# GpSimd in program order in attention, the fifth tile's branch inside w2's first tile, and the maxima's steps listed anew

## The chip, the cores and the metric

The kernel runs on one core of one Trainium2 chip. The time is the device time of one execution in microseconds (us), and the time before is the median of three runs, 1415.97 us (1415.85 to 1416.66).

The core's engines have queues of their own and run side by side: TensorE (PE; its weight loads are PEld), VectorE (DVE), ScalarE (ACT), GpSimd (POOL) and SyncE (SP), which issues most DMAs. A wait between engines is a semaphore.

## What is computed

```python
x = A_x                                     # [1, 2048, 448]
g = sigmoid((x * gate_w).sum(-1, keepdims=True))
# a: attention, 16 heads of 28
q, k, v = (x @ wqkv) split into heads
a = softmax(q @ k.T * 28**-0.5) @ v @ wo
# b: two of eight experts a token, w1[e]: 448 x 1792, w2[e]: 1792 x 448
topk_idx = argsort(-(x @ w_gate))[:, :2]
gates = softmax(topk_val)
for e in range(8):
    b += (gates * (topk_idx == e)).sum(-1) * (silu(x @ w1[e]) @ w2[e])
out = g * a + (1 - g) * b
```

## The kernel before

**Precision.** A product of fp32 numbers is made of three fast matmuls: each operand is split into a high part (a rounded copy, by ScalarE) and a low part (the rest, by GpSimd or VectorE), and high x high, high x low and low x high are added up. So w1, w2, the tokens and the hidden values all have a copy and a subtraction of their own: `w1h`, `w1l`, `w2h`, `w2l`, `xeh`, `xel`, `hh`, `hl`.

**Stages.** First q, k, v and the router are computed and written to DRAM (to about 119 us). Then come the eight experts, in falling order of their token counts (loop at L859). Then attention over 256 units of 4 heads x 512 queries x 128 keys (L1160 on), and the projection by `wo`.

**One expert.** Its tokens are gathered into four tiles of 128 slots, and for experts 0 to 5 a fifth, smaller one (64 slots or fewer, `CTS[e][4]`), which holds tokens only if the count is over 512. The 1792 hidden rows are done in two halves (`hf`) of seven row tiles each. In a half, w1 comes first: 7 row tiles x 2 halves of the slots x 11 matmuls, 154 in all (L898). Then w2: one output tile for each of the four token tiles, 21 matmuls each, 84 in all (L948). In half 1 the tokens of the next expert are transposed in groups of four matmuls (`turn_x`, L749) between w2's matmuls, two groups in the first tile (behind its 6th and 15th) and one in each later one.

**Accumulators.** Two PSUM banks, `acc0` and `acc1`, are used in turn: `accumulator()` switches to the other one and returns it, `other_accumulator()` returns the one that isn't in use and switches nothing. The transpositions of `turn_x` also go to the other one.

**The fifth tile.** Its w1 part is the end of the second slot half. Its w2 part, `last_slots` (L819), stands in a branch `tc.If(cnt > 512)` (L935): 14 matmuls (28 passes, L825) into one bank, two copies of it by ScalarE (L831), and in half 1 two additions by GpSimd (L833) and two DMAs (L834). Before, the branch stands ahead of w2's first tile.

**The maxima.** Attention needs the largest score of each query first. This work is put into the experts' stage, between TensorE's other matmuls: 1024 blocks of 128 queries x 512 keys (L112). A generator hands them out in steps. A step writes six blocks to the PSUM tile `pm` (six banks, one buffer), and a seventh to the accumulator that is not in use, if it got it as a spare bank; VectorE takes the maximum of each (L126 for the seventh, L132 for the others in two instructions). When 16 query columns of a head group are ready, the maxima are gathered (`mg`, L141), and the next step that gets a bank uses it to transpose and store them (`store_max`, L148) and has six blocks.

**Where the steps stand.** The table `STEPS` gives, for each expert and half, the numbers of the matmuls in w1 (1 to 154) and in w2 (1 to 84) behind which a step comes (`behind`, L853). A negative number is a step without a spare bank.

**Who sets the order.** In the experts' stage PE, DVE, ACT and POOL run in program order (`MANUAL_E`), and SP's order is set by the scheduler. In attention only PE and DVE are in program order (L1074); the scheduler orders ACT, POOL and SP.

**Attention.** `scores` computes a unit's scores (L695) into a bank `ps1` and three banks `ps3`, and ScalarE takes the exponentials (L1091, L1092), three units ahead of `values` (L1101), which adds up P x V. Sixteen units of 128 keys make a pass of four heads over 512 queries; `kt` counts the 16. At the end of a pass the result is copied (`osb`, L1105) and `spread_sums` sends the sums through DRAM by eight GpSimd DMAs (L1048, L1051). In the next pass `divide` uses them at kt 6 to 9. `fetch_routed` (L1005) gathers the two expert results of 128 tokens by two GpSimd DMAs (L1009), `routed` adds them up by VectorE at kt 12, and `split_wo` loads and splits a quarter of `wo` (L1001 to L1003).

Of the kernel before, what the change touches and what calls it, by code (L numbers as in the profile page):

```python
# [20 lines left out]
BUSY = 20  # L21


A, B, C = (17, 50, 83, 116, 149), (17, 50, 83, 116, -154), (-4, 28, 61, 94, -124, 148)
F, G, T = (18, 38, 57, 76), (13, 32, 50, 68), (-11, -25, 39, 59, 76)
STEPS = [((C, F), (A, T)), ((A, G), (C, T)), ((A, G), (C, T)), ((B, F), (B, T)), ((B, F), (B, T)), ((B, F), (B, T)),
         ((A, F), (A, T)), ((A, F), ((-13, 39, 72, 105, 138), (9, 28, 47, 67)))]

S, D, H, DH, E, FF = 2048, 448, 16, 28, 8, 1792
NT = S // 128  # L30
# [24 lines left out]
def tile_gated_mha_moe(ctx: ExitStack, tc: tile.TileContext, x, xT, wv, wqk, wo, w1, w2, out):  # L55
# [106 lines left out]
    def tail_twice(xt):  # L162
        nc.scalar.activation(xt[:, D:512], xt[:, 384:D], AF.Copy)
# [24 lines left out]
    def step(bank):  # L188
        if bank and flush:
            store_max(*flush.pop(0), bank)  # L190
        elif bank:
            spare.append(bank)
        next(ms, None)
        spare.clear()
# [505 lines left out]
    with ExitStack() as pb:  # L700
# [36 lines left out]
        def accumulator():  # L737
            turn[0] ^= 1
            return ps.tile([128, 512], F32, name=f"acc{turn[0]}")

        def other_accumulator():
            return ps.tile([128, 512], F32, name=f"acc{turn[0] ^ 1}")
# [75 lines left out]

        def last_slots(e, hf, hs, y):  # L819
            n, w = CTS[e][4], D // 2  # L820
            py = accumulator()
            for f in range(NH):
                w2r = w2t[e * NF + hf * NH + f][2]
                for c in range(2):
                    nc.tensor.matmul(py[64 * c:64 * c + n, 0:w], hs[f][2][:, 0:n], w2r[:, c * w:(c + 1) * w],  # L825
                                     start=f == 0, stop=f == NH - 1)
            r0 = e * CPAD + 512
            yo = sb.tile([128, D], F32, name="yo") if hf else y
            for c in range(2):
                rw = slice(64 * c, 64 * c + n)  # L830
                nc.scalar.activation(yo[rw, 0:w], py[rw, 0:w], AF.Copy)  # L831
                if hf:
                    nc.gpsimd.tensor_tensor(yo[rw, 0:w], yo[rw, 0:w], y[rw, 0:w], op=ALU.add)  # L833
                    nc.gpsimd.dma_start(ys_d[r0:r0 + n, c * w:(c + 1) * w], yo[rw, 0:w])  # L834
# [18 lines left out]
        def behind(places, i):  # L853
            if i in places:
                step(other_accumulator())
            elif -i in places:
                step(None)

        for e in range(E):  # L859
            CT, HC = CTS[e], CAPS[e] // 2  # L860
            later = CTS[e + 1] if e + 1 < E else []
            if len(CT) == 5:
                cnt = nc.values_load(cnt_i[0:1, 0, e:e + 1], min_val=0, max_val=S)
# [5 lines left out]
            ysb = [None] * 5  # L869
            for hf in range(2):  # L870
                hs = []
                lag = None
                w1_steps, w2_steps = STEPS[e][hf]
                for f in range(NH):
# [48 lines left out]
                    xeh, xel = x_tiles()  # L923

                base = e * NF + hf * NH
                for n_k, k in enumerate((4, 0, 1, 2, 3)):
                    if k == 4:
                        if hf == 0 and len(CT) == 5:
                            ysb[4] = sb.tile([128, D], F32, name="ysb", bufs=5)
                        if (e, hf) == (E - 1, 1):  # L930
                            spilled()

                            nc.scalar.activation(sb.tile([128, 1], F32, name="warm", bufs=1), ident[:, 0:1], AF.Exp)
                        if len(CT) == 5:
                            with tc.If(cnt > 512):  # L935
                                last_slots(e, hf, hs, ysb[4])
                        for f in range(NH):
                            fetch_w2(base + f + 9)
                    n = 128
                    cs = slice(k * 128, k * 128 + n)  # L940
                    if k < 4:
                        py = accumulator()
                    i = 0
                    for f in range(NH if k < 4 else 0):
                        hh, hl, ht = hs[f]
                        w2h, w2l, w2r = w2t[base + f]
                        for a, b in ((hh, w2h), (hh, w2l), (hl, w2h)):
                            nc.tensor.matmul(py[:n, 0:D], a[:, cs], b, start=i == 0, stop=i == 3 * NH - 1)  # L948
                            i += 1
                            behind(w2_steps, 3 * NH * (n_k - 1) + i)  # L950
                            if (e, hf, n_k) == (E - 1, 1, 4) and i in (1, 10):
                                first_scores(i == 10)
                        if hf == 1 and e + 1 < E and (f == 1 or f == 4 and n_k == 1):
                            j = n_k if f == 1 and n_k > 1 else f // 4
                            if j < len(later):
                                turn_x(xgs[j], j, later[j], xeh, xel)
                    if hf == 0 and n_k:

                        r0 = e * CPAD + 512 if n_k == 1 else NMAIN + (3 * e + n_k - 2) * 128
                        nc.sync.dma_start(ys_d[r0:r0 + 128], zero_d)  # L960
                    if hf == 0:
                        if k < 4:
                            ysb[k] = sb.tile([128, D], F32, name="ysb", bufs=5)
                            nc.scalar.activation(ysb[k], py[:, 0:D], AF.Copy)
                        if e + 1 < E:
                            for j in {0: (0, 1), 4: ()}.get(n_k, (n_k + 1,)):
                                if j < len(later):
                                    xgs.append(gather(e + 1, j))
                            for j in {0: (), 1: (0, 1)}.get(n_k, (n_k,)):
                                if j < len(later):  # L970
                                    tail_twice(xgs[j][:later[j]])
                    elif k < 4:
                        r0 = e * CPAD + k * 128
                        yo = sb.tile([128, D], F32, name="yo")
                        nc.scalar.activation(yo, py[:, 0:D], AF.Copy)
                        nc.gpsimd.tensor_tensor(yo, yo, ysb[k], op=ALU.add)
                        nc.sync.dma_start(ys_d[r0:r0 + n], yo)

                    free = {0: ((e * NP + 4, 0),), 1: ((e * NP + NP, 0), (e * NP + NP + 1, 2))}[hf]
                    for p, at in free:  # L980
                        if n_k == at:
                            split_w1_high(p, WHOLE)
                            split_w1_low(p, WHOLE)
# [87 lines left out]
                r += n  # L1071
                p += n

    ctx.enter_context(tc.manual_schedule(engines={mybir.EngineType.PE, mybir.EngineType.DVE}))  # L1074
    todo = []
    b1s, halves, ygs = {}, {}, {}
    units = [(g, qc, kt) for g in range(NG) for qc in range(4) for kt in range(NT)]
# [124 lines left out]
```

## Time and profile before

| what | us |
|---|---|
| median of 3 runs | 1415.97 |
| profiled execution | 1420.36 |
| its span | 1418.6 |
| PE busy | 1402.2 |
| ACT busy | 913.5 |
| DVE busy | 799.6 |
| POOL busy | 645.3 |

The span is the stretch from the first to the last instruction of the program; the rest of an execution lies around it. PE counts as busy for 99% of it, but the ends of matmuls are modelled in the profile, and a matmul begins before the one ahead of it has ended. So small losses are to be read from the distance between the starts of two matmuls, and the rows of time (start in us, duration in us, engine, line, operation, output<-input, partitions x elements, and in brackets the idle time before it and who ended it) serve for that.

### The profile page before, as it was taken

How to read it: one execution, taken by the hardware profiler on the slowest of the kernel's cores; microseconds unless marked ns; L12 is line 12 of the kernel's file. 1: busy time of each engine (PE TensorE's matmuls, PEld its weight loads, DVE VectorE, ACT ScalarE, POOL GpSimd, SP SyncE). 2: the span in 40 equal slices, each digit the busy share in tenths (PEclk: the TensorE clock that was granted, in tenths of full speed). 3: DMA queues.
4: the chain of work that ended last, by engine and by line, in shares of the span. 5: the costliest groups of instructions: out<-in, count | busy, mean ns of one | idle time of the engine just before them, and what ended most of it. 6: DMA issues, size and time to landing. Idle time of an engine off the chain costs nothing. (4 is left out here: it accounts for less than half of the span.)

```text
span 1418.6 us, 28718 instructions
## 1 busy us (share of the span) xinstructions
PE 1402.2 (99%) x11028; PEld 935.7 (66%) x11028; DVE 799.6 (56%) x911; ACT 913.5 (64%) x1531; POOL 645.3 (45%) x682
## 2 busy tenths in 40 slices
PE   9999999999999999999999999999999999999999
PEld 8888888878878888888888887333333333333348
DVE  5736777777877787778888886022231122311136
ACT  5335355355445543654445434899999999999981
POOL 2224587487478666875777636221121122121120
PEclk9999999999999999999999999999999999999999
DMA  9886552343233234323442211311421331142103
GB/s 340 285 282 229 154 164 61 107 138 92 77 119 119 64 113 124 110 64 105 136 124 83 70 59 38 87 44 47 124 75 42 95 84 49 42 126 63 33 22 120
DMA packets 106685, 152.81 MB, mean 108 GB/s; under 512 B 17926, under 2 KB 77523, under 8 KB 106032
## 3 DMA queue, kind: packets, MB, share of 16 engines
q1 hardware_dynamic: 97392, 129.86, 29.7%
q0 software_dynamic: 9008, 20.83, 5.1%
q8 instruction: 89, 1.46, 0.4%
q14 instruction: 52, 0.43, 0.1%
q10 hardware_dynamic: 144, 0.23, 0.1%
HBM read 115.99 MB, written 38.02 MB: 109 GB/s over the span
## 5 line engine op out<-in xcount | busy, mean ns | idle before, releaser
L132 DVE TENSOR_REDUCE mp<-pm 128x3 f32<-128x1536 f32 (+3 forms) x307 | 520.0, 1736 | 43.7 <-PE pm L112 43.7
L1092 ACT ACTIVATE P<-ps 128x1536 f32<-128x1536 f32 x254 | 367.9, 1448 | 0.1
L1101 PE MATMUL po<-P,V 128*32 128x512 f32 x2032 | 270.6, 604 | 0.0
L898 PE MATMUL acc<-xeh,w1h 128*128 128x256 f32 (+6 forms) x880 | 252.5, 296 | 0.0
L898 PE MATMUL acc<-xeh,w1l 128*128 128x256 f32 (+6 forms) x880 | 246.4, 289 | 1.1 <-POOL w1l L730 0.9
L695 PEld LDWEIGHTS ps<-Q,Kh 29*128 29x128 f32 x2032 | 78.1, 183 | 216.2 <-ACT P L1091 213.3
L767 POOL TENSOR_TENSOR w2l<-w2r,w2h 128x448 fp32r<-128x448 f32 x112 | 129.2, 1154 | 161.2 <-ACT w2h L761 122.3
L695 PE MATMUL ps<-Q,Kh 29*128 29x512 f32 x2032 | 189.6, 443 | 3.2 <-ACT P L1091 3.0
L898 PE MATMUL acc<-xel,w1h 128*128 128x256 f32 (+6 forms) x660 | 189.6, 287 | 0.0
L898 PEld LDWEIGHTS acc<-xeh,w1h 128*128 128x128 f32 x880 | 165.7, 188 | 25.4 <-issue 25.2
L948 PE MATMUL acc<-w2h,hh 128*128 128x448 f32 x448 | 170.8, 381 | 2.1 <-ACTq L935 1.8
L898 PEld LDWEIGHTS acc<-xeh,w1l 128*128 128x128 f32 x880 | 165.9, 189 | 4.7 <-POOL w1l L730 2.8
L948 PE MATMUL acc<-w2h,hl 128*128 128x448 f32 x448 | 166.8, 372 | 0.5 <-POOL hl L776 0.5
L948 PE MATMUL acc<-w2l,hh 128*128 128x448 f32 x448 | 166.4, 372 | 0.0
L1105 DVE COPY osb<-po 128x512 f32<-128x512 f32 x16 | 11.1, 692 | 264.3 <-PE po L1101 195.7
L902 ACT ACTIVATE hf<-acc 128x256 f32<-128x256 f32 (+6 forms) x224 | 86.3, 385 | 113.9 <-PE acc L898 98.4
L1048 POOL DMA_DIRECT2D sum_d<-osb x64 | 32.3, 522 | 270.5 <-DVE osb L1105 254.5
L1091 ACT ACTIVATE P<-ps 128x512 f32<-128x512 f32 x254 | 151.8, 598 | 5.3 <-PE ps L695 2.3
L730 POOL TENSOR_TENSOR w1l<-w1r,w1h 128x512 fp32r<-128x512 f32 (+1 forms) x88 | 138.1, 1569 | 29.5 <-ACT w1h L724 22.4
L776 POOL TENSOR_TENSOR hl<-hf,hh 128x512 fp32r<-128x512 f32 x112 | 143.9, 1291 | 0.0
L126 DVE TENSOR_REDUCE mp<-acc 128x1 f32<-128x512 f32 x111 | 76.8, 692 | 105.5 <-PE acc L112 98.0
L898 PEld LDWEIGHTS acc<-xel,w1h 128*128 128x128 f32 x660 | 124.5, 189 | 0.9 <-issue 0.7
(214 smaller groups left out, 1989.6 us busy)
## 6 DMA issues: line engine op xcount, KB each, us to landing
w2r<-in_w_dram SPq DMA_DIRECT2D x112, 224.0 KB
w1r<-in_w_dram SPq DMA_DIRECT2D x56, 384.0 KB
ys_d<-zero_d SPq DMA_DIRECT2D x32, 224.0 KB
qkh_d<-hi SPq DMA_DIRECT2D x28, 256.0 KB
qkl_d<-lo SPq DMA_DIRECT2D x28, 256.0 KB
w1r<-in_w_dram SPq DMA_DIRECT2D x112, 64.0 KB
ys_d<-yo SPq DMA_DIRECT2D x32, 224.0 KB
v_d<-v_s SPq DMA_DIRECT2D x16, 256.0 KB
```

The lines of the kernel that those rows point to most:

```text
L126: nc.vector.tensor_reduce(mp[:, o:o + 1], banks[0], axis=AX.X, op=ALU.max)
L132: nc.vector.tensor_reduce(mp[:, (o + lo) % 256:(o + lo) % 256 + hi - lo], pm[:, lo:hi], axis=AX.X, op=ALU.max)
L695: nc.tensor.matmul(banks[j], k[rw, ks], q[rw, c], start=i == 0, stop=i == 2)
L730: nc.gpsimd.tensor_tensor(l[:, :, half], r[:, :, half], h[:, :, half].bitcast(F32), op=ALU.subtract)
L767: nc.gpsimd.tensor_tensor(w2l, w2r, w2h.bitcast(F32), op=ALU.subtract)
L776: nc.gpsimd.tensor_tensor(hl, hf32, hh[:, 0:512].bitcast(F32), op=ALU.subtract)
L898: nc.tensor.matmul(pu[:, 0:HC], a, b[:, cs], start=i == 0, stop=i == len(mms) - 1)
L902: nc.scalar.activation(hf32[:, hs_], pu[:, 0:nh], AF.Silu)
L948: nc.tensor.matmul(py[:n, 0:D], a[:, cs], b, start=i == 0, stop=i == 3 * NH - 1)
L1091: nc.scalar.activation(P[:, 0], p1, AF.Exp, scale=SCALE)
L1092: nc.scalar.activation(P[:, 1:4], p3, AF.Exp, scale=SCALE)
L1101: nc.tensor.matmul(po[32 * j:32 * j + 32], v[:, kt % 8, 32 * j:32 * j + 32], P[:, j] if n > 1 else P[j], start=kt == 0, stop=kt == NT - 1)
```

## The change

Three edits. `STEPS` is listed anew, 152 places instead of 154. The fifth tile's branch moves from ahead of w2's first tile to behind its third matmul, and its product goes to the accumulator that is not in use instead of the next one in turn; so w2's first tile takes the accumulator that the fifth tile had, and every later tile the other one of the two. The whole split of a pair of w1 (`split_w1_high` and `split_w1_low` with WHOLE) and the loads of w2 stand ahead of the branch in the program. And in attention GpSimd keeps the program's order.

```diff
-A, B, C = (17, 50, 83, 116, 149), (17, 50, 83, 116, -154), (-4, 28, 61, 94, -124, 148)
-F, G, T = (18, 38, 57, 76), (13, 32, 50, 68), (-11, -25, 39, 59, 76)
-STEPS = [((C, F), (A, T)), ((A, G), (C, T)), ((A, G), (C, T)), ((B, F), (B, T)), ((B, F), (B, T)), ((B, F), (B, T)),
-         ((A, F), (A, T)), ((A, F), ((-13, 39, 72, 105, 138), (9, 28, 47, 67)))]
+STEPS = [
+    (([17, 50, 83, 116, 148], [13, 32, 51, 70]), ([7, 39, 72, -100, -124, 148], [-11, -25, 39, 59, 76])),
+    (([17, 50, 83, 116, 149], [18, 38, 57, 76]), ([17, 50, 83, 116, 148], [-11, -25, 39, 59, 76])),
+    (([17, 50, 83, 116, 149], [18, 38, 57, 76]), ([17, 50, 83, 116, 148], [-11, -25, 39, 59, 76])),
+    (([17, 50, 83, 116, 149], [18, 38, 57, 76]), ([17, 50, 83, 116, 148], [-11, -25, 39, 59, 76])),
+    (([17, 50, 83, 116, 149], [18, 37, 56, 75]), ([17, 50, 83, 116, 148], [-11, -25, 39, 59, 76])),
+    (([17, 50, 83, 116, 149], [18, 37, 56, 75]), ([17, 50, 83, 116, 148], [-11, -25, 39, 56, 75])),
+    (([17, 50, 83, 116, 149], [18, 37, 56, 75]), ([17, 50, 83, 116, -149], [-11, -25, 39, 56, 75])),
+    (([17, 50, 83, 116, 148], [15, 34, 53, 72]), ([-12, 39, 72, 105, 138], [9, 28, 47, 67])),
+]
...
         def last_slots(e, hf, hs, y):
             n, w = CTS[e][4], D // 2
-            py = accumulator()
+            py = other_accumulator()
...
+                def fifth():
+                    if len(CT) == 5:
+                        with tc.If(cnt > 512):
+                            last_slots(e, hf, hs, ysb[4])
+
                 for n_k, k in enumerate((4, 0, 1, 2, 3)):
...
-                        if len(CT) == 5:
-                            with tc.If(cnt > 512):
-                                last_slots(e, hf, hs, ysb[4])
                         for f in range(NH):
                             fetch_w2(base + f + 9)
...
                             i += 1
+                            if n_k == 1 and i == 3:
+                                fifth()
                             behind(w2_steps, 3 * NH * (n_k - 1) + i)
...
-    ctx.enter_context(tc.manual_schedule(engines={mybir.EngineType.PE, mybir.EngineType.DVE}))
+    ctx.enter_context(tc.manual_schedule(
+        engines={mybir.EngineType.PE, mybir.EngineType.DVE, mybir.EngineType.Pool}))
```

## The prediction

> **What bounds the kernel now.** I read the busy time by stage first, then who makes TensorE wait, then the order of time around each place that the change touches.
>
> ```profile
> core 0: us, PE busy (x) PEld busy (x) DVE busy (x) ACT busy (x) POOL busy (x), PEclk, DMA share, GB/s
> 119.00:883.00 764.00, 756.28 (x5142) 629.64 (x5140) 600.62 (x498) 370.37 (x909) 518.22 (x454) 1.00 0.35 104
> 903.00:1377.00 474.00, 473.35 (x4968) 164.60 (x4967) 105.39 (x185) 471.58 (x497) 91.38 (x148) 1.00 0.24 64
> ```
>
> From 119 to 883 us (experts) TensorE is busy 756 of 764 us; from 903 to 1377 (attention) ScalarE is busy 471.6 of 474. The first stage follows TensorE's stream and what holds it up, the second follows the exponentials. All three edits work on small holes in these two streams.
>
> ```profile
> PE pm L112 <- DVE mp L132: 2.3, 5, 0.6
> PE pm L112 <- DVE lo L609: 0.9, 1, 0.9
> PE acc L898 <- POOL w1l L730: 0.9, 2, 0.7
>   PEld pm L112: 2.6, 9
> ```
>
> The last row, from the list of who waited on tile mp, adds nine weight loads of the maxima that also waited for VectorE. Matmul ends are modelled, so I measure a wait as the distance between starts, against an undisturbed place. Undisturbed, with a spare bank (seven score blocks, TensorE then VectorE):
>
> ```profile
> 177.28 0.29 PE L898 MATMUL acc<-xel,w1h 128*128 128x288 f32 x1
> 177.41 0.29 PE L898 MATMUL acc<-xeh,w1l 128*128 128x288 f32 x1
> 177.64 0.49 PE L112 MATMUL acc<-khg,qg 28*128 28x512 f32 x1
> 178.30 0.40 PE L898 MATMUL acc<-xeh,w1h 128*128 128x288 f32 x1
> 178.54 0.29 PE L898 MATMUL acc<-xel,w1h 128*128 128x288 f32 x1
> 178.17 0.69 DVE L126 TENSOR_REDUCE mp<-acc 128x1 f32<-128x512 f32 x1 [1.56 <-PE acc L112]
> 178.77 3.42 DVE L132 TENSOR_REDUCE mp<-pm 128x3 f32<-128x1536 f32 x2
> ```
>
> From 177.41 to 178.54 are 1.13 us where two pitches of 0.13 would be 0.26: a step costs TensorE 0.87 us. VectorE has read all of its banks at 178.77 + 3.42 = 182.19, 4.55 us after the step began. The tile pm has one buffer, so the next step must lie some 4.7 us behind. Two blocked places, each behind a step without a spare bank (six blocks):
>
> ```profile
> 394.09 0.29 PE L898 MATMUL acc<-xel,w1h 128*128 128x276 f32 x1
> 394.31 0.49 PE L112 MATMUL acc<-khg,qg 28*128 28x512 f32 x1
> 394.65 0.73 PE L112 MATMUL pm<-khg,qg 28*128 28x512 f32 x6
> 395.54 0.29 PE L898 MATMUL acc<-xeh,w1h 128*128 128x276 f32 x1
> 585.06 0.73 PE L112 MATMUL pm<-khg,qg 28*128 28x512 f32 x6
> 586.10 0.44 PE L948 MATMUL acc<-w2h,hh 128*128 128x448 f32 x1 [0.31 <-ACTq L935]
> 586.58 0.37 PE L948 MATMUL acc<-w2h,hl 128*128 128x448 f32 x1
> 586.79 0.37 PE L948 MATMUL acc<-w2h,hh 128*128 128x448 f32 x1
> 587.40 0.60 PE L749 MATMUL acc<-ident,xg 128*128 128x128 f32 x4
> 587.76 0.45 PE L948 MATMUL acc<-w2h,hh 128*128 128x448 f32 x1
> 589.40 0.73 PE L112 MATMUL pm<-khg,qg 28*128 28x512 f32 x6 [0.39 <-DVE mp L132]
> ```
>
> The first takes 395.54 - 394.09 = 1.45 us, 0.32 more than undisturbed. The second shows the rule for six blocks: 589.40 - 585.06 = 4.34 us. So after a seven-block step TensorE needs 4.7 us of other work, after a six-block step 4.35, or it waits.
>
> **The maxima's steps.** With 0.13 us a w1 matmul (about 0.12 in the last experts, whose tiles have 256 columns instead of 288: an estimate by columns), 0.207 a w2 matmul (586.58 to 586.79), 0.87 for the step itself and 0.4 for a group of four transpositions (587.40 to 587.76), the old lists miss these distances at five kinds of places. (a) 24 matmuls behind a six-block step (-4 to 28, -124 to 148; three halves): 24 x 0.13 + 0.87 = 3.99 against 4.35; six places, 0.32 in the row above and less where w1 is wider, 1.5 in sum. (b) 32 to 50: 18 x 0.207 + 0.87 = 4.60 against 4.7, two places, 0.2. (c) The last w1 step to -11 in w2: 0.39 by the row for each of experts 3 to 5; for expert 6, 5 x 0.12 + 11 x 0.207 + 0.4 + 0.87 = 4.15 against 4.7; 1.7 in sum. (d) 76 to 17 of the next half: 8 x 0.207 + 17 x 0.12 + 0.87 = 4.57 against 4.7; nine places, 1.2. (e) Last expert, 76 to -13 and -13 to 39: 4.09 against 4.7 and 3.99 against 4.35, 1.0. Sum 5.6 us.
>
> In the new lists most of these are gone: 75 to 17 has 9 x 0.207 + 17 x 0.12 + 0.87 = 4.77; 148 to -11 has 6 x 0.125 + 11 x 0.207 + 0.4 + 0.87 and the branch, some 4.6 against 4.7; 72 to -12 has 12 x 0.207 + 12 x 0.12 + 0.87 = 4.79. Left are -100, -124 and 148 in expert 0 (24 to 28 matmuls apart, 0.7 in sum), some 0.2 at -11 in experts 3 to 5, 0.2 in expert 6, 0.24 at -12 to 39, and I add 0.3 for the transpositions of maxima (L148), which now come 16 to 19 matmuls behind a step and need its VectorE work too: 1.6. The pair -25 to 39 is the same in both lists and left out. Saved 4.0.
>
> Counted out over the 1024 blocks, the old lists hold 154 steps, the new 152, since 118 instead of 110 have a spare bank: 2 x 0.87 = 1.7 saved. The first step moves from place 4 to 17, past the one wait for `low`:
>
> ```profile
> 120.87 0.80 PE L112 MATMUL pm<-khg,qg 28*128 28x512 f32 x6 [0.94 <-DVE lo L609]
> ```
>
> Thirteen matmuls later it has nothing to wait for: 0.9 saved. Together 6.6 us.
>
> What is late next is GpSimd.
>
> ```profile
> L776 POOL TENSOR_TENSOR hl<-hf,hh 128x512 fp32r<-128x512 f32 x112 | 143.9, 1291 | 0.0
> L767 POOL TENSOR_TENSOR w2l<-w2r,w2h 128x448 fp32r<-128x448 f32 x112 | 129.2, 1154 | 161.2 <-ACT w2h L761 122.3 <-PE acc L898 25.9 <-PE pm L112 12.9
> L730 POOL TENSOR_TENSOR w1l<-w1r,w1h 128x512 fp32r<-128x512 f32 x66 | 85.3, 1293 | 24.8 <-ACT w1h L724 22.4 <-PE acc L898 0.9 <-PE pm L112 0.9
> 862.53 0.39 PE L898 MATMUL acc<-xeh,w1l 128*128 128x256 f32 x1 [0.70 <-POOL w1l L730]
> ```
>
> In a row of w1 that also splits the next pair, GpSimd has 1.29 + 1.15 + 1.29 = 3.73 us of work, and TensorE in the last experts only 22 x 0.12 + 0.87 x 5/7 = 3.26. There a wait saved early in w1 comes back as a wait for w1l. I give back the (d) places of experts 4 to 7 (seven of 0.15) and what (e) saved (0.75): 1.8. Without any of it the stage would gain 6.6, with all w1 gains from expert 3 on lost about 4. I take 4.8.
>
> **The branch.** Twelve times a fifth tile's branch moves behind three matmuls of w2's first tile. Six copies for half 0, two a run, say that three experts take it; three don't.
>
> ```profile
> 146.38 2.87 PE L825 MATMUL acc<-w2r,ht 128*64 128x224 f32 x28
> 149.18 0.47 PE L948 MATMUL acc<-w2h,hh 128*128 128x448 f32 x1
> L831 ACT ACTIVATE ysb<-acc x6: 351/352/353, 149.3 to 350.2; 64x224 f32<-64x224 f32 x2, 52x224 f32<-52x224 f32 x2, 40x224 f32<-40x224 f32 x2
> ```
>
> Not taken, before: 586.10 - 585.06 = 1.04 us against 0.66 (177.64 to 178.30), so 0.38. In the compiled order the skipped path still waits until TensorE's last matmul has ended, now the third of the tile (0.37 us long, next due after 0.21), so 0.3 to 0.5 again: I take no difference, between 0.38 gained and 0.3 lost at each of six. Taken, the fifth tile sits in the other accumulator and its two copies (0.35 us each) must end before the first transposition in half 1, only three matmuls (0.6) later: 0.2 lost in each of three, 0 in half 0, where the next user comes fifteen matmuls later; bounds 0 and 0.7. Behind it on ScalarE and GpSimd now stands the whole pair's split, which goes ahead of the branch: neither copy is due while it runs. SP's w2 loads still wait for these matmuls, as before. Lost: 0.6.
>
> **GpSimd in attention.** By the compiled orders, before, the gathers of b stand two units ahead, six of them and two loads of wo at the start; after, two gathers at kt = 1 of each unit, behind the sums of the unit before, and wo in unit 5. The first microseconds of attention, ScalarE, GpSimd, and two stretches by engine:
>
> ```profile
> 895.88 1.45 ACT L1092 ACTIVATE P<-ps 128x1536 f32<-128x1536 f32 x1
> 899.08 0.60 ACT L1091 ACTIVATE P<-ps 128x512 f32<-128x512 f32 x1 [1.75 <-remote]
> 902.03 0.60 ACT L1091 ACTIVATE P<-ps 128x512 f32<-128x512 f32 x1 [0.85 <-PE ps L695]
> 893.28 0.97 POOL L1009 DMA_INDIRECT yg<-ys_d,slot_i  x1 [2.78 <-DMA ys_d<-yo]
> 896.00:903.00 7.00, 4.46 (x47) 1.64 (x43) 1.14 (x2) 4.35 (x5) 4.88 (x6) 1.00 0.71 200
> 905.00:917.00 12.00, 12.00 (x132) 4.36 (x132) 0.00 (x0) 11.85 (x13) 0.00 (x0) 1.00 0.00 1
> ```
>
> ScalarE loses 2.6 us exactly while these transfers keep the DMA engines at 0.71, and nothing right after. With a quarter of them there I take 2.0 saved; bounds: 2.6 saved, and 2 lost if gathers behind the sums disturb later units. VectorE will wait at split_wo in unit 5, but its next duty is the division at kt = 6, some 10 us later, and routed comes at kt = 12, 20 us after its gathers: cover enough.
>
> **Sum.** -4.8 + 0.6 - 2.0 = -6.2 us. The profiled execution took 1420.36 us (span 1418.6): 1414.2. It lies 4.39 above the median of the three runs (1415.97), to which I carry the difference: **1409.8**.
>
> **Rivals.** First, the stall at 896 isn't made by GpSimd's transfers (the first two gathers, which stay, begin before it): attention gives 0, 1411.8. Second, GpSimd paces the experts so far that from expert 3 on only the saved steps in w2 count, about 2 us less, and attention gives 0: 1413.8. For it speaks the row at 862.53, against it that the list has only two such waits, 0.9 us in all. Third, slower: branches inside an open tile.
>
> ```profile
> q8 instruction: 89, 1.46, 0.4%
> ```
>
> 0.4% of 16 engines' 1418.6 us over 89 loads is 1.0 us for each load of instructions; if every one of the twelve branches exposed one, 12 us more, 1421.8. It decides from 6.2 / 12 = 0.5 us a branch. Against it: the same branches stand in the trace now at 0.38 (not taken), and taken w2 starts at 149.18, before the fifth tile's passes have ended (146.38 + 2.87). The Trainium skill's Runtime: NRT & Kernel Launch, Instruction fetch mechanics, says that a taken branch whose target lies outside the two pages held makes the sequencer fetch the page first; by that rule the third rival comes about wherever a page border falls inside a branch. The trace shows no branch with such a delay, so the rule gets only this rival's chance. Fourth, that the lists are shifted by the first tile's new inner gap and all fit: 1407.5.
>
> **How the numbers follow.** Forecast 0.48, first rival 0.20, second 0.14, third 0.10, fourth 0.08. The range takes in the first, second and fourth and the bounds of the branch: 1406 to 1415.5. A measurement of this kernel can tell 0.2%, 2.8 us, from no change: 1413.1 is the border. Forecast, fourth and most of the first lie below: faster 0.73, same 0.17, slower 0.10.
>
> **What would show it.** Two fewer steps of L112 (152); the wait on `low` gone; the rows pm <- DVE mp and mp's weight loads at a third or less; waits for w1l longer in experts 5 to 7; the skipped branch at about 0.4 inside the tile; the two holes of ScalarE at 897 and 901 gone or down to one. Wrong would make it: a hole of 1 us at each branch, attention not shorter, or w1l waits that grow by more than 2 us.

## The result, and the profile after

The changed kernel took 1413.72 us (median of 14 runs, 1411.89 to 1414.42), the kernel before, measured beside it, 1416.47 (14 runs, 1415.85 to 1417.84): ratio 0.9978, 95% interval 0.997 to 0.9987, or 2.75 us less. Forecast was 1409.8, 6.2 us less than the 1415.97 known then. The profiled execution of the changed kernel took 1413.67 us, within 0.1 us of that median. The one of before, on which the prediction was built, took 1420.36, which is above every one of the 14 timed runs of before. That turns out to be the point of this case.

The stretches by engine of the changed kernel's trace; columns as in the prediction:

```profile
119.00:880.00 761.00, 755.47 (x5146) 626.03 (x5145) 600.35 (x502) 369.95 (x911) 518.92 (x454) 1.00 0.34 105
892.00:899.00 7.00, 7.00 (x76) 2.63 (x72) 1.14 (x2) 7.00 (x8) 0.00 (x0) 1.00 0.12 36
```

The experts' stage ends some 3 to 4 us earlier. In the first microseconds of attention (896 to 903 us) ScalarE was busy 4.35 of 7.00 us before; in the same part of the changed kernel (892 to 899) it is busy all 7.00, GpSimd is idle there and the DMA engines' share fell from 0.71 to 0.12.

Who made TensorE wait in the experts' stage of the changed kernel (total us, times, longest):

```profile
PE acc L904 <- POOL w1l L736: 1.1, 3, 0.7
PE acc L755 <- ACTq L934: 0.9, 3, 0.3
PE acc L118 <- ACT ht L910: 0.8, 1, 0.8
PE pm L701 <- DVE mp L138: 0.3, 1, 0.3
PE acc L956 <- PEq L787: 0.3, 1, 0.3
PE acc L956 <- POOL hl L782: 0.2, 1, 0.2
PE pm L118 <- DVE mp L138: 0.2, 1, 0.2
```

The steps' waits for mp fell from 2.3 us to 0.2, the wait for `low` is gone, the wait for w1l grew from 0.9 to 1.1. Three waits are new: 0.9 us of the transpositions for ScalarE, 0.8 us of one step for ht, and 0.3 us of attention's first scores for mp. VectorE's reductions of the steps' six common banks, first of before, then of the changed kernel:

```profile
L132 DVE TENSOR_REDUCE mp<-pm 128x3 f32<-128x1536 f32 (+3 forms) x307 | 520.0, 1736 | 43.7 <-PE pm L112 43.7
```

```profile
L138 DVE TENSOR_REDUCE mp<-pm 128x3 f32<-128x1536 f32 (+2 forms) x304 | 515.7, 1738 | 32.3 <-PE pm L118 32.3
```

With two reductions a step, 304 is 152 steps, and 307 one short of 154: the two steps fewer are there.

To compare many traces I use three distances between starts in the timeline. **Experts**: from the first w1 matmul (119.24 us in the trace of before, 119.18 after) to the last w2 matmul (888.29, 884.37). **Attention**: from there to the last long exponential (1376.02, 1368.17). **End**: from there to the end of the span. I also use the **excess**: by how much the distances of the long exponentials exceed 1.90 us (an undisturbed one is 897.49 - 895.59 = 1.90 in a quotation below), summed over those that exceed it by over 0.015.

| us | before | after | difference |
|---|---|---|---|
| experts | 769.05 | 765.19 | -3.86 |
| attention | 487.73 | 483.80 | -3.93 |
| excess in it | 5.97 | 1.48 | -4.49 |
| end | 42.54 | 43.69 | +1.15 |
| profiled execution | 1420.36 | 1413.67 | -6.69 |
| median of 14 runs | 1416.47 | 1413.72 | -2.75 |

The two traces differ by 6.7 us, close to the forecast. The runs differ by 2.75. Some 4 us of what the traces show was never in the timed runs, and the experiments had to find which.

### The profile page after: what moved, and what is told of

Same layout as the page of the kernel before. It is cut to its first block, busy times and chain, and to the rows that moved or that the text cites. A ratio compares the mean times of both kernels' runs of the same rounds, so it can differ in the third digit from the quotient of the medians.

```text
span 1411.9 us, 28709 instructions
## 1 busy us (share of the span) xinstructions
PE 1399.9 (99%) x11028; PEld 931.1 (66%) x11028; DVE 799.5 (57%) x915; ACT 912.3 (65%) x1531; POOL 641.0 (45%) x682
## 5 line engine op out<-in xcount | busy, mean ns | idle before, releaser
L138 DVE TENSOR_REDUCE mp<-pm 128x3 f32<-128x1536 f32 (+2 forms) x304 | 515.7, 1738 | 32.3 <-PE pm L118 32.3
L132 DVE TENSOR_REDUCE mp<-acc 128x1 f32<-128x512 f32 x118 | 81.6, 692 | 117.5 <-PE acc L118 110.4
```

The lines of the kernel that those rows point to most:

```text
L132: nc.vector.tensor_reduce(mp[:, o:o + 1], banks[0], axis=AX.X, op=ALU.max)
L138: nc.vector.tensor_reduce(mp[:, (o + lo) % 256:(o + lo) % 256 + hi - lo], pm[:, lo:hi], axis=AX.X, op=ALU.max)
```

## The experiments

Two theories stood at the start. **T**: the experts' stage gains its 3 to 4 us in every run; ScalarE's holes at 897 to 902 us belong to the one profiled execution, so GpSimd's order gives nothing. **R**, the prediction's step: the holes are in every run, and the gain was lost elsewhere. The runs came on several chips, which I call by letters: A is that of the result (its number is not on record, so it may be one of the others), B, C, D and E those of the experiments. In the median before took 1420.8 to 1421.5 on B and C, 1416.4 to 1416.5 on A and D, and 1420.18 in the one run on E. Each ratio is to before on the same chip. On which chip the prediction's trace of before was taken is not on record either.

### Single edits, chip B

Before again, unchanged:

> The kernel before, unchanged: a second profiled execution. Theory T: the holes of ScalarE at 897 to 902 us (1.75 + 0.85), at 938 and at 1060 us belong to the one execution that was profiled (1420.36 us, 4.4 above the median of its runs); a second one, if it takes 1416 to 1417, has no hole over 0.3 us there, and the distances of the exponentials' starts exceed 1.90 us by about 1.5 us in sum over attention, not 6.0. Its experts' stage (last step of the maxima) still ends at about 883.7. Rival R, which is the prediction's step: the stall is in every run, the two holes are at 897 to 902 again, 2.0 to 2.6 us together. Times: ratio 1.000 by both.

Measured: 1420.9 us, ratio 1.0001 (0.9992 to 1.001). Experts 768.60, attention 488.35, excess 6.18. The holes are there again: 2.73, 0.30 and 0.85 us too much behind the exponentials of 895.48, 900.11 and 902.31. T falls in the form in which it was stated: this is another execution, on another chip, with the same holes, and here all runs are as slow as the profiled one.

Before with GpSimd in program order alone:

```
-    ctx.enter_context(tc.manual_schedule(engines={mybir.EngineType.PE, mybir.EngineType.DVE}))
+    ctx.enter_context(tc.manual_schedule(
+        engines={mybir.EngineType.PE, mybir.EngineType.DVE, mybir.EngineType.Pool}))
```

> Before, with nothing but GpSimd's program order in attention. T: on the ordinary runs it saves nothing, and the 1.16 us longer end of the changed kernel (last exponential to end 42.29 us against 41.13) may come with it: ratio 1.000 to 1.0008 (1416.5 to 1417.6 us). R: the prediction's 2.0 us are saved in every run: ratio 0.9986 (1414.5 us), and if it made the whole 4.5 us by which attention is shorter in the two traces, 0.9968.

Measured: 1417.93, ratio 0.9978 (0.9969 to 0.9987). Experts 768.80, attention 484.80, excess 3.94 without a hole in the first ten microseconds. On this chip R is right: 2.9 us, even more than the 2.0 forecast.

The changed kernel without that edit (lists and branch stay):

```
-    ctx.enter_context(tc.manual_schedule(
-        engines={mybir.EngineType.PE, mybir.EngineType.DVE, mybir.EngineType.Pool}))
+    ctx.enter_context(tc.manual_schedule(engines={mybir.EngineType.PE, mybir.EngineType.DVE}))
```

> The changed kernel with GpSimd's order in attention put back. T: the 3.9 us that the experts' stage gained stay, the end is as before: ratio to before 0.997 to 0.998 (1412.5 to 1413.7 us), as fast as the whole change or up to 1.2 us faster. R: it loses the 2.0 us and more: ratio 0.9992 (1415.7 us) or above.

Measured: 1416.67, ratio 0.9969 (0.9957 to 0.9981), 4.2 us less than before. Experts 765.27, attention 487.61, so 3.3 us come from the experts and the holes stay.

Before with the new lists alone (`STEPS` replaced, nothing else):

> Before, with the new lists of the maxima's steps alone: the branch stands ahead of the tile and GpSimd is as before. T: the experts' stage gains most of its 3.9 us here, and the branch's place is worth 0.6 us either way: ratio 0.9970 to 0.9978 (1412.2 to 1413.4 us). The prediction's step gives 4.8 us: 1411.7. R (the lists give little in ordinary runs, their gain is taken back by GpSimd in the experts): ratio 0.9986 or above.

Measured: 1417.88, ratio 0.9982 (0.9973 to 0.9991), 2.95 us less. Experts 765.78. Its waits of TensorE name a cost that the whole change does not have:

```profile
PE acc L954 <- ACT ht L910: 3.2, 6, 0.5
PE acc L118 <- ACT ht L910: 1.1, 1, 1.1
```

With the new lists and the branch still ahead of the tile, the first matmul of w2 waits six times 0.5 us for ScalarE's ht (in before six times 0.3, put down to the branch, the row below). Behind three matmuls that wait is gone.

```profile
PE acc L948 <- ACTq L935: 1.8, 6, 0.3
```

### The whole change and the branch, chip C

> The whole change again. In the first pair of runs before took 1416.47 and the changed kernel 1413.72, on the chip of the single edits before took 1420.83. Theory H (the single edits add up where before shows the holes at 897 to 902): on a chip on which before takes about 1420.8 the whole change gives lists and branch (ratio 0.9969, -4.2 us) and GpSimd's order (0.9978, -2.9 us) together, 0.994 to 0.9955 (1413 to 1414.5 us, as in the first runs); on one on which before takes about 1416.5 it gives 0.998 again. Rival O (the edits overlap: each of them takes away the same delay): 0.9965 to 0.998 whatever before takes.

Measured: 1414.95, ratio 0.9957 (0.9944 to 0.9971), 5.9 us less than before's 1420.87. Experts 765.28, attention 485.33, excess 4.55. The ratio lies just outside H's range (0.994 to 0.9955) and outside O's (0.9965 to 0.998), and its interval reaches into both. The stretches decide: the experts are as short as with lists and branch (765.27), and attention nearly as short as with GpSimd's order alone (484.80). So the edits add up on a chip with holes, to 5.9 us instead of the 7.1 of H, and the forecast of -6.2 is met there.

Before with the branch alone (behind three matmuls of the first tile, other accumulator; old lists, old order):

```
-            py = accumulator()
+            py = other_accumulator()
...
-                        if len(CT) == 5:
-                            with tc.If(cnt > 512):
-                                last_slots(e, hf, hs, ysb[4])
...
+                            if n_k == 1 and i == 3:
+                                fifth()
```

> Before, with the fifth tile's branch and accumulator alone; old lists, old order of GpSimd. The prediction charges it 0.6 us: ratio 1.0004. The difference between the two runs with the new lists (1416.67 with the branch moved, 1417.88 without) would make it 1.2 us of gain: 0.9992. A load of instructions exposed at every branch, the prediction's third rival: 1.008.

Measured: 1421.01, ratio 1.0003 (0.9994 to 1.0012): 0.14 us by the medians, within the uncertainty. Experts 769.75, against 768.60 to 769.05 in four traces of before. So alone it costs a little or nothing, as the prediction had it (0.6); with the new lists it is worth about 0.5 us in the experts (765.78 to 765.27, one trace each, where the traces with both edits spread from 764.84 to 765.63). That this is the wait for ht is likely and not shown: with the branch alone the 1.8 us of before's row are gone as well, and nothing is gained.

The changed kernel with the branch behind nine matmuls and four steps of expert 0 two or three places later:

```
-                            if n_k == 1 and i == 3:
+                            if n_k == 1 and i == 9:
...
-    (([17, 50, 83, 116, 148], [13, 32, 51, 70]), ...
+    (([17, 53, 86, 118, 150], [13, 32, 51, 70]), ...
```

> The changed kernel with the branch behind nine matmuls instead of three, and in the first half of expert 0 the steps 50, 83, 116, 148 at 53, 86, 118, 150. In the changed kernel's trace the transpositions wait three times 0.3 us for ScalarE, which stands in the skipped branch, and step 50 of expert 0 waits 0.8 us for ht. If both waits are late work that six matmuls or three cover, 1.7 us less than the whole change (ratio to it 0.9988); if they only come back as waits for w1l of GpSimd, no difference.

Measured: 1414.57, ratio 0.9952 (0.9938 to 0.9965); experts 765.20, so no difference from the whole change. The waits moved instead of going away:

```profile
PE acc L831 <- ACT xf L759: 1.7, 3, 0.6
...
PE acc L118 <- ACT ht L910: 0.3, 1, 0.3
```

Now the fifth tile's own matmuls (L831, the three times that the branch is taken) wait 1.7 us for the copies of a transposition, where the transpositions had waited 0.9 us for the skipped branch. Neither of the two outcomes expected names this.

Before once more, on chip C:

> The kernel before, a third profile. H: if this chip runs before at 1416 to 1417, ScalarE has no hole of over 0.5 us between 893 and 905 us and the distances of the exponentials' starts exceed 1.90 us by under 2.5 us in sum; if it runs it at about 1420.8, both holes are there and the sum is about 6. Rival: the holes are there either way, and the 4 us between the chips lie in another stage (their places will show in the times at which w1, w2 and the exponentials start).

Measured: 1419.88; experts 768.64, attention 487.73, excess 5.82. The first hole is there (2.72 us). The second, 0.85 to 0.9 in the other two traces of before, is not: 0.21 and 0.19 in its place. 1.00 us is lost behind the exponential of 1058.77, as in the other two (0.92 and 0.95). A third trace of before with holes, still none without.

The second hole may be a consequence of the first and not of the transfers. In the four traces so far in which its exponential waits 0.8 us or more for TensorE's scores on chips B and C (before again, without GpSimd's edit, the lists alone, the branch alone), the granted clock behind the first stop is 0.57 to 0.70 over 4 us; in this trace, without the second hole, it stays at 1.00 from 897 to 905 us. The prediction's trace has the second hole at a recorded clock of 1.00, so this is not settled.

### A chip without holes, chip D

Three variants of the changed kernel, and before itself. The diff of the first, with before's bundle of gathers and loads of wo; the second leaves out every change of `split_wo`:

```
-        if g == 1 and qc == 1 and kt % 4 == 1:
+        if g == 1 and qc == 1 and kt in (9, 13):
             split_wo(kt // 4)
-        if kt == 1:
+        if kt == 1 and u not in (1, 2):
             fetch_routed(u)
-        if kt == 12:
+        if kt == 12 and u:
             b1s[u] = routed(u)
+        if n == 8:
+            b1s[0] = routed(0)
+            fetch_routed(1)
+            fetch_routed(2)
+            split_wo(0)
+            split_wo(1)
```

> The changed kernel with before's bundle of GpSimd transfers (four gathers and two loads of wo in a row) put back, but eight key tiles into the first unit of attention (about 905 to 915 us) instead of three. Theory B: the bundle itself stops ScalarE, so the two holes follow it: none at 893 to 902, 2.5 and 0.8 us or so within 10 us behind the bundle's first gather, 2.5 to 4 us more than the whole change (ratio 0.998 to 0.9985 where that gives 0.9957). Rival S: the holes belong to the first microseconds of attention (buffers and instructions used for the first time) and GpSimd's order only happened to be changed there: no hole behind the bundle, ratio as of the whole change.

> As the kernel before this one, but with the four gathers alone, the two loads of wo where the change has them. B with the gathers as the cause: the same holes (2 to 4 us in sum). B with the loads of wo as the cause: none over 0.3 us. S: none either.

The third, on the version with the branch behind nine matmuls:

```
-        if kt == 1:
+        if kt == 4:
             fetch_routed(u)
-        if kt == 12:
+        if kt == 13:
             b1s[u] = routed(u)
```

> The version with the branch behind nine matmuls, and each unit's two gathers at its fifth key tile instead of its second, the sums of b1 at the fourteenth. In the whole change's second trace ScalarE loses 0.6 us at 1014.59, 0.6 at 1138.98 and 0.2 to 0.3 at 1166, 1196 and 951, each while the gathers run beside SP's loads of keys, values or queries. If the meeting of the two makes these losses, attention is 1.5 to 2.5 us shorter than with the branch behind nine matmuls (ratio 0.9935 to 0.9942 where that gave 0.9952); if any gather costs that, wherever it is, no difference.

> The kernel before, once more, for the case that this chip runs it at 1416 to 1417. Theory H: then the holes at 893 to 905 us are under 0.5 us; rival: they are there as on the other chips, and the difference lies in another stage. On a chip that runs it at 1420.8 it adds a third pair of holes of 3.5 to 4 us in sum.

Measured: before took 1416.35 here. The bundle 1413.7, ratio 0.998 (0.9971 to 0.9989), attention 483.81, excess 1.50; the gathers alone 1412.53 (one run), 483.80, 1.47; gathers at the fifth key tile 1413.07, ratio 0.9976 (0.9966 to 0.9986), 483.91, 1.55. No hole in any of them. The last run is the one that settles it: **before itself** took 1416.11 and its attention is 483.76 with an excess of 1.42. Experts 768.61, end 42.52, as on the other chips. The whole difference between the chips is in attention: 487.73 in the last trace on chip C against 483.76, 4.0 us. By the excess it is 4.4, of which 3.1 stand between 895 and 906 us and 1.0 at 1059.

Before on chip C, around the first hole (start, duration, engine, line, in brackets the idle time and what ended it):

```profile
895.47 0.95 POOL L1009 DMA_INDIRECT yg<-ys_d,slot_i  x1 [0.30 <-issue]
895.59 1.45 ACT L1092 ACTIVATE P<-ps 128x1536 f32<-128x1536 f32 x1
...
895.86 0.75 PE L695 MATMUL ps<-Q,Kh 29*128 29x512 f32 x8
...
896.43 0.40 PE L695 MATMUL ps<-Q,Kl 28*128 28x512 f32 x4
896.72 0.95 POOL L1009 DMA_INDIRECT yg<-ys_d,slot_i  x1 [0.30 <-issue]
...
899.52 0.60 ACT L1091 ACTIVATE P<-ps 128x512 f32<-128x512 f32 x1 [2.48 <-remote]
```

The same kernel at the same place on chip D:

```profile
895.53 0.95 POOL L1009 DMA_INDIRECT yg<-ys_d,slot_i  x1 [0.30 <-issue]
895.59 1.45 ACT L1092 ACTIVATE P<-ps 128x1536 f32<-128x1536 f32 x1
...
895.93 0.74 PE L695 MATMUL ps<-Q,Kh 29*128 29x512 f32 x8
...
896.50 0.41 PE L695 MATMUL ps<-Q,Kl 28*128 28x512 f32 x4
896.78 0.95 POOL L1009 DMA_INDIRECT yg<-ys_d,slot_i  x1 [0.30 <-issue]
...
896.99 0.60 ACT L1091 ACTIVATE P<-ps 128x512 f32<-128x512 f32 x1
897.49 1.45 ACT L1092 ACTIVATE P<-ps 128x1536 f32<-128x1536 f32 x1
```

The same gathers start within 0.06 us of each other, the scores that the exponential needs are done at 896.43 + 0.40 = 896.83 and 896.91. On D the exponential follows at 896.99, on C at 899.52. The row says `remote`, as if no engine of this core had ended the wait. But the semaphore that the exponential waits for is TensorE's, and the trace records when it was raised: on D at 896.91, with the end of the matmuls, on C at 899.44, 2.61 us after their recorded end and 0.08 before the exponential. So ScalarE stops because TensorE's signal comes late. Whether only the signal is late or the matmuls too, the trace can't tell, since the ends of matmuls are modelled. The stretch of 12 us on C and on D, last two columns the DMA engines' share and GB/s:

```profile
893.00:905.00 12.00, 9.33 (x96) 3.40 (x96) 1.14 (x2) 9.16 (x11) 6.92 (x8) 1.00 0.52 154
```

```profile
893.00:905.00 12.00, 12.00 (x128) 4.27 (x128) 1.14 (x2) 11.90 (x14) 6.98 (x8) 1.00 0.53 154
896.00:903.00 7.00, 7.00 (x77) 2.73 (x80) 1.14 (x2) 6.93 (x8) 4.59 (x6) 1.00 0.73 213
```

The transfers, their share and their rate are equal; ScalarE is busy 9.16 us on one chip and 11.90 on the other. The last row is the prediction's stretch, on D: the share is 0.73 and ScalarE is busy 6.93 of 7.00 us. The share of the DMA engines, by which the prediction argued, does not tell the two apart.

One thing does. When a gather lands, it leaves 16 records of its semaphore in an undisturbed stretch. On D each of the six gathers has its 16; on C they have 5, 4, 3, 3, 11 and 16. So where ScalarE stops, the recording loses records too, and so it is in all nine traces with a hole of over 1.5 us, that of the prediction included (5, 5, 3, 5, 16, 16): four or five gathers of the row have lost records. In the other ten no gather has lost more than two. Whether the recording has a part in the stop, or only suffers with the engines, is a rival that no run here tests.

### What makes the holes where they are, chips C and E

> The kernel with the bundle eight key tiles into attention, on another chip. If before takes about 1420.8 there: theory B (the bundle stops ScalarE where the chip lets it) gives the two holes within 10 us behind its first gather, ratio 0.998 to 0.9985; rival S (they belong to the first microseconds) gives no hole and 0.9955 to 0.996. If before takes about 1416.4: no hole and 0.998, as in the run before, by both.

> The four gathers alone at that place. On a chip with holes: 2 to 4 us if the gathers make them, under 0.3 if the loads of wo are needed for them.

The third moves the two loads of wo alone (`if n == 8: split_wo(0); split_wo(1)`):

> The two loads of wo alone at that place. On a chip with holes: under 0.3 us if the gathers make them, 1 to 3 us if the loads of wo do.

> Each unit's gathers at its fifth key tile and the branch behind nine matmuls. On the chip where before took 1416.35 it had the same attention as the changed kernel (excess of the starts 1.55 us against 1.48 to 1.50) and ratio 0.9976. On a chip with holes: if gathers beside SP's loads cost the 0.2 to 0.6 us at 1014, 1139, 1166, 1196, attention's excess falls from 4.6 to under 2.5 and the ratio is 0.993 to 0.9945; if any gather costs it, 0.995 to 0.9958.

Measured, on chip C again (before 1421.46): the bundle 1420.44, ratio 0.9993 (0.9983 to 1.0002), attention 488.87, excess 8.39; gathers alone 1419.9 (one run), 490.19, 8.88; loads of wo alone 1414.69 (one run), 484.81, 3.57; gathers at the fifth key tile 1414.36, ratio 0.995 (0.9933 to 0.9966), 485.19, 4.37. The first two lose more than was expected (the bundle's ratio was to be 0.998 to 0.9985, the gathers' loss 2 to 4 us): 4.10 us in one distance of the exponentials alone, behind 892.59 and 892.77. The six gathers in a row, without wo:

```profile
890.15 0.97 POOL L1019 DMA_INDIRECT yg<-ys_d,slot_i  x1 [2.78 <-DMA ys_d<-yo]
...
891.42 0.95 POOL L1019 DMA_INDIRECT yg<-ys_d,slot_i  x1 [0.30 <-issue]
...
892.67 0.96 POOL L1019 DMA_INDIRECT yg<-ys_d,slot_i  x1 [0.30 <-issue]
892.77 1.45 ACT L1103 ACTIVATE P<-ps 128x1536 f32<-128x1536 f32 x1
...
893.93 0.95 POOL L1019 DMA_INDIRECT yg<-ys_d,slot_i  x1 [0.30 <-issue]
...
895.19 1.01 POOL L1019 DMA_INDIRECT yg<-ys_d,slot_i  x1 [0.30 <-issue]
896.50 0.95 POOL L1019 DMA_INDIRECT yg<-ys_d,slot_i  x1 [0.30 <-issue]
897.40 0.60 ACT L1102 ACTIVATE P<-ps 128x512 f32<-128x512 f32 x1 [3.18 <-remote]
...
898.77 1.45 ACT L1103 ACTIVATE P<-ps 128x1536 f32<-128x1536 f32 x1 [0.77 <-remote]
```

Two gathers and the two loads of wo:

```profile
889.66 0.97 POOL L1019 DMA_INDIRECT yg<-ys_d,slot_i  x1 [2.77 <-DMA ys_d<-yo]
890.93 0.95 POOL L1019 DMA_INDIRECT yg<-ys_d,slot_i  x1 [0.30 <-issue]
891.88 1.21 POOL L1011 DMA_DIRECT2D wo_r<-in_wo_dram  x2
```

No exponential behind these is late. So on such a chip a row of gathers makes holes of 0.8 to 3.2 us, with the loads of wo or without, and two gathers with the two loads do not. The latter also move less, an estimate of 0.9 MB against 1.4 (a gather is 128 rows of 1792 bytes, a load 224 KB), so the runs don't separate the kind of transfer from the number in a row. And these runs did not do what their diffs say: nothing holds GpSimd back to a key tile, it ran ahead, and the row came at 890 to 897 us instead of 905 to 915, on D as well. So theory B and rival S are not yet told apart. The fourth run shows the same slip. First the gathers at 1013 us with the edit, then without it (the branch behind nine matmuls):

```profile
1013.62 1.01 POOL L1019 DMA_INDIRECT yg<-ys_d,slot_i  x1 [0.30 <-issue]
1014.94 0.97 POOL L1019 DMA_INDIRECT yg<-ys_d,slot_i  x1 [0.30 <-issue]
```

```profile
1013.71 1.02 POOL L1019 DMA_INDIRECT yg<-ys_d,slot_i  x1 [0.30 <-issue]
1015.03 0.97 POOL L1019 DMA_INDIRECT yg<-ys_d,slot_i  x1 [0.31 <-issue]
```

The edit moved nothing, so this run says nothing on the rest of the excess on chip C (4.4 to 4.7 us against 1.5 on D). The second trace of the whole change, on C, does: of its 4.55 us of excess 3.7 lie around the pairs of gathers, from 2 us before a pair's first to 5 behind it, against 0.7 of the 1.48 on A. Three pairs, at 951.8, 1166.3 and 1196.8 us, lose 0.31 to 0.33 while no packet of SP's queue starts in the 4 us behind the pair's first, so the expectation above, that each meets SP's loads, misreads these. The two of 0.6 (1014.59 and 1138.98) do have SP's loads beside or just ahead of them. So a pair of gathers loses something on this chip by itself; whether SP's loads add to it stays open.

To put the row at another time it must stand behind something that GpSimd waits for, the sums of unit 0:

```
-        if kt == 1:
+        if kt == 1 and u not in (2, 3):
             fetch_routed(u)
-        if kt == 12:
+        if u == 1 and kt == 1:
+            b1s[1] = routed(1)
+            fetch_routed(2)
+            fetch_routed(3)
+        if kt == 12 and u != 1:
             b1s[u] = routed(u)
```

> The changed kernel with the gathers of units 1, 2 and 3 in a row behind the sums of unit 0 (from about 921 us), where the order of GpSimd holds them back; the first unit's two stay at 889. Theory B: on a chip that runs before at about 1420.8 ScalarE stops 1 to 2 us behind the third gather of this row, 2.5 to 4.5 us in sum between 922 and 935, and nowhere at 889 to 902. Rival S: no hole there over 0.5 us. On a chip that runs before at 1416.4: none by either.

Measured, on chip E: 1421.27 against 1420.18 for before (one run each), attention 491.70.

```profile
921.64 1.02 POOL L1019 DMA_INDIRECT yg<-ys_d,slot_i  x1 [0.30 <-issue]
...
922.96 0.97 POOL L1019 DMA_INDIRECT yg<-ys_d,slot_i  x1 [0.30 <-PE ps L701]
...
924.23 0.95 POOL L1019 DMA_INDIRECT yg<-ys_d,slot_i  x1 [0.30 <-issue]
...
925.49 0.95 POOL L1019 DMA_INDIRECT yg<-ys_d,slot_i  x1 [0.30 <-issue]
925.99 0.60 ACT L1102 ACTIVATE P<-ps 128x512 f32<-128x512 f32 x1 [1.07 <-PE ps L701]
...
930.45 0.60 ACT L1102 ACTIVATE P<-ps 128x512 f32<-128x512 f32 x1 [2.52 <-remote]
```

The row has six gathers, 921.64 to 928.16. The exponentials lose 1.11 and 2.56 us in the two stops shown, 3.7 in sum, as theory B forecast, and at 889 to 902 they have no hole. The holes follow the row of gathers; they have nothing to do with the start of attention. The missing records moved with the row as well: its gathers have 5, 6, 5, 2, 3 and 16 landing records of 16, the pair at 890 has all.

Another 2.6 us (0.49, 1.55 and 0.57), 6.4 in sum from 921 to 939, follow when the row is over, and were not forecast. There the granted clock (the third figure from the end of the row below) is 0.65, and the late exponentials wait for TensorE's scores:

```profile
931.00:940.00 9.00, 8.90 (x68) 3.09 (x72) 0.76 (x2) 6.51 (x8) 0.00 (x0) 0.65 0.10 26
```

## Why the prediction was right and wrong

**The step that failed** is the third term, "ScalarE loses 2.6 us exactly while these transfers keep the DMA engines at 0.71 ... I take 2.0 saved", together with the line under the sum: the profiled execution "lies 4.39 above the median of the three runs (1415.97), to which I carry the difference". Half of its mechanism is right: where the holes are, they follow the row of gathers, and GpSimd's program order breaks the row up, which saves 2.9 us on chip B (interval of the ratio 0.9969 to 0.9987). The other half, that the load on the DMA engines makes them, is not: on D the same load stops nothing. So it happens only on some chips, and the three runs were most likely taken on one where it does not: chip D runs before at 1416.35 with an attention of 483.76, the changed kernel's own trace has 483.80. There the term is 0, not -2.0. The prediction named the 4.39 us and left them unexplained. They could have been found: the excess of the exponentials in that trace is 5.97 us, 4.5 more than in a trace without holes. A hole that has the size of the gap between the profiled execution and the runs must be asked first whether the runs have it. That the chip of the result is of the kind of D is inferred, from before's 1416.47 and the changed kernel's 1.48 us of excess; no trace of before was taken on it.

**The experts' stage** was forecast at -4.8 + 0.6 = -4.2. Measured: 768.60 to 769.05 in four traces of before, and 764.84 to 765.63 (mean 765.23) in the twelve traces with the new lists and the moved branch, -3.5 from the mean of the four, 768.73. By parts: the lists alone -2.8 to -3.3 (765.78, one trace), the branch with them some -0.5. The two steps fewer are there, the wait for `low` is gone, mp's direct waits fell to a tenth. But the weight loads that waited for mp, 2.6 us before, did not get fewer:

```profile
  PEld pm L118: 2.7, 9
```

That part of the 4.0 us was not saved. Against it GpSimd took back 0.2 us in the list of waits and not 1.8. Step 50 of expert 0 waits 0.8 us for ht, which was not forecast. At the skipped branch itself "I take no difference" held: in the changed kernel's trace the fourth matmul of the tile starts 0.51 us behind the third (445.52 to 446.03), 0.30 more than the pitch of 0.207, against 0.38 before. But the transpositions wait 0.9 us where the branch is *not* taken, while the prediction charged it to the taken one: it looked only at the next matmul and not at ScalarE, which stands in the branch. By the starts it is more: the first transposition comes 0.64 us behind the matmul ahead of it (491.46 to 492.10), before 0.21 (493.54 to 493.75).

**The end** is not in the sum. Seven traces with GpSimd's old order have 42.40 to 42.91 us, twelve with the new one 42.40 to 43.69, 0.3 more in the mean (42.94 against 42.61). The two ranges overlap, so whether the order causes it stays open.

With these sizes the sum for a chip without holes is -3.5 + 0 + 0.3 = -3.2 (measured -2.75; the ratio's interval is -1.8 to -4.2). On chip C attention went from 487.73 to 485.33, on B before had 488.35: -2.4 to -3.0, and the sum is -5.6 to -6.2 (measured -5.9 on C).

**The rivals.** The first gave attention 0 and so 1411.8, 4.2 us less than before; but its reason is refuted on the chips with holes, where the holes move with GpSimd's transfers. The second gave 1413.8, 2.2 us less, and is the nearest of all to what was measured. That is luck: its attention of 0 is right for another reason, and its cause, GpSimd as the experts' pace, is not seen (1.1 us of waits for w1l, and 3.5 us gained where it allows 2.2). The third, 1.0 us for each branch, would have shown as 12 us in the branch alone; that run has a ratio of 1.0003, and the changed kernel's page has the same row of instruction loads as before:

```profile
q8 instruction: 89, 1.46, 0.4%
```

The rule that the prediction took from the Trainium skill's Runtime: NRT & Kernel Launch, Instruction fetch mechanics, is that a taken branch whose target lies outside the two pages held must first fetch the target's page; the runs show no branch with such a delay. The fourth needs waits that vanish, which they did not.

## What to carry to other kernels

Before a stall of a profiled execution is booked as a gain, compare that execution's time with the runs that the result will be measured against: if it lies above them by about what its stalls add up to, the stalls are probably missing in the runs, and the forecast must weigh the case in which their removal gives nothing. When an instruction is moved on an engine that runs ahead, ask which wait holds it at its new place; without one it moves in the program only. And when a branch moves, the engines that take no part in its next instruction also stand in it: look who waits for them.

## What the runs showed of the hardware

The same program with the same transfers has, on some chips, stops of ScalarE that others do not have: with 154 GB/s and a DMA share of 0.52 to 0.53 in both, ScalarE stood 2.48 us at 897 us on chip C and not at all on chip D. The stops of 0.8 to 3.2 us come behind the third or fourth of a row of indirect gathers from GpSimd (1.25 us apart), move with that row (897, 894 and 928 us), and do not come with two gathers and two plain loads of wo. Smaller losses come with a mere pair of gathers: on chip C 0.3 to 0.6 us in the changed kernel, and 1.00 us at 1059 in before (gathers at 1057.68 and 1059.31), where the trace on D loses nothing. So three in a row is no threshold.

In the stop ScalarE waits for TensorE's signal. On chip C it was raised at 899.44, 2.61 us behind the recorded end of the scores (896.83), on D at 896.91, with their end (896.91). No load of instructions falls into the hole: on C the loads next to it start at 886.41 and 903.98 us. In the same microseconds the trace on C lacks most landing records of the gathers (5, 4, 3 and 3 of 16), on D none. What delays the signal, whether the recording has a part in it, and what is different on those chips, no run here shows.

In six of the nine traces with a stop of over 1.5 us the granted clock of TensorE fell behind it for 4 to 8 us, to 0.50 or 0.57 over the lowest 2 us. In the other three, among them that of the prediction, it stayed at 1.00 on record. Nowhere else from 120 to 1366 us was it below 0.97 over 2 us, in any of the 19 traces.
